# Inverse transform of a gated convolution in three classes of time points, with the filter taken through the path of the activations and a gate ahead of the weight loads

## The chip, the cores and the metric

The kernel runs on 1 core of one Trainium2 chip. The metric is the device time of one execution in microseconds (us). The time before is the median of 3 runs, 191.38 us (190.6 to 192.84). The profile is of one further execution.

## What is computed

Attention first, then a convolution whose result is gated by two projections. B = 4 batches, H = 8 heads, S = 768 positions, D = 64, model width 512. Heads 0, 2 and 6 attend causally to everything, the other five to 4 sink positions and a window of 64. The convolution is circular over the 768 positions, with one filter per channel, and is computed on the spectrum.

```python
scores = scale * np.matmul(q, k.transpose(0, 1, 3, 2))
scores = np.where(mask[None, :, :, :], scores, -1000000000.0)
a = np.exp(scores - max); a = a / sum
x = np.matmul(a, v)                       # -> [B, S, 512]
...
x1, x2, x3 = split(x @ w_proj, 3)         # w_proj 512 x 1536
X2 = np.fft.rfft(x2, n=S, axis=1)
H = np.fft.rfft(filter_fft, n=S, axis=0)[None, :, :]
x2_conv = np.fft.irfft(X2 * H, n=S, axis=1)
return (x1 * x2_conv * x3) @ w_out        # [4, 768, 512] float32
```

## The kernel before, in words

**Order.** The order of all work is written out by hand in two strings of words. `AHEAD` (L121) is what runs before a branch that asks whether the heads have the expected kinds; `FAST` (L126) is the rest. Each word is the name of a small function; the kernel calls them one by one (L1738), and every engine works through its own instructions in that order, with semaphores between engines. `@4` names a PSUM bank, `/v`, `/s` and `/p` name VectorE (DVE), ScalarE (ACT) or GpSimd (POOL). Helpers `ev` (L969, a copy out of PSUM or a cast), `two` (L977, an operation on two tensors) and `scale` (L1157) take the engine from that letter, so that many operations share the lines 971, 973, 975 and 978.

**Attention.** Sixteen pairs of heads (n = 0 to 15, four per batch) are loaded by `lq`, `lk`, `lv` on SP's queue, cast (`cq`, `ck`, `cv`), turned (`T`, `E`), multiplied (`sc`, L1452), masked by a bias matmul (`sb`, L1465, n below 4) or by a multiplication (`mk`), exponentiated on ACT (`ex`, L1471), multiplied by the values (`at`, L1516) and normalized (`rec`, `nm`, L1533; twice by ACT, L1530). Buffers of a head pair are two or three deep.

**Transform forwards.** The normalized heads are folded over the half length (`fd`, `fe`) and over sixths (`fA`, `fS`, `fb`, `fr`, L1561), and three matmuls per half (`W`, L1569 to L1573) give 2 x 384 frequencies per channel, copied out by `We`. Heads are also turned for the two projections (`tn`, `te`): by PE (L1589) for the head pairs in `TURNED_BACK`, by a DMA for the others. `X` (L1620) multiplies the spectrum by the middle third of w_proj, so that frequencies lie on the partitions, and `Xe` copies it out.

**The filter.** `lfilt` (L1236) loads it on POOL's queue, as `lw` (L1244) and `lwo` (L1249) load the weights; their place in the order is all that sets when they start. `fold0` and `fold1` fold it, 18 matmuls of 512 columns (`F`, L1265) with the table G as weights give its spectrum with frequencies on the partitions, and `H` (L1272, L1274, with two copies by DMA, L1288 and L1292) scales it into HAB.

**Product and inverse.** `pa`, `pb`, `pc` multiply X by HAB into P; for one tile of three the halves of X have to be exchanged by two DMAs (`sw`, L1645). For each of four blocks of 128 channels, `c` (L1685) makes two chains of three matmuls with 384 columns, one even and one odd under a shift by half the length. `ce` copies the one out on ACT, and `cv` adds and subtracts the other on DVE (L1696). `y` multiplies by x1, `g` (L1674, L1678) by x3; x1 and x3 come from `x1`, `x3` (L1655), and `o` (L1712) with `oe` and `st` gives the output.

```python
INVERSE = (((1, 0, 3), (1, 1, 4), (2, 1, 5)), ((0, 0, 0), (0, 1, 1), (2, 0, 2)))
```

The table Gi of the inverse is the transpose of the table G: 18 transposes on PE (`Gt`, L1227) and three copies (`Ge`). G itself is mixed from one wave by four operations on DVE (`Gm`, L1188). `blank` words are matmuls on zeros (L1041) near the start.

Of the kernel before, what the change touches and what calls it, by code (L numbers as in the profile page):

```python
# [114 lines left out]
TURNED_BACK = (0, 1, 2, 3, 4, 5, 6, 7, 14, 15)  # L115
# [3 lines left out]
BLANKS = (5, 2, 2, 2, 2, 2, 2, 2, 2, 2, 2, 2, 2)  # L119

AHEAD = """  # L121
lflag lk0 lq0 lk1 lq1 mblank want tcol fcol0 table sin0 fcol1 blank0@6 tfrac quarter mtab0 par turns other angle
ident mtab1 wrap size sin cos
# [3 lines left out]
ones1 ones2 mtab3 blank5@0 lq2 lk2 blank10@1 ck0/v skew0/s lv0 parb skew1/p G32/s T0.1@2 xp0 cq0/v lk3 blank6@3  # L127
mtab2 E0.1/v lv1 blank8@4 Gk1/s lv3 blank7@5 Gm00 btab G31/p blank1@6 ck1/v kz1 lq3 T0.0@7 lk4 alt blank3@0 Gm2
cq1/s G30/p Gh0 lq4 T1.1@1 Gm01 kz0 lv2 E0.0/s G00/v T1.0@3 G01/p Gm1 cq2/s lk6 E1.1/v sc0.1@4 sb0.1 lq6 ck2/p
sc0.3@6 ex0.1 Gh1 E1.0/v sc0.4@0 ones0 kx1/p sb0.4 lk5 sb0.3 T2.1@2 ex0.4 kz2 lk7 sc0.0@4 E2.1/v lq5 cv0/p sb0.0  # L130
Gt1@3 ex0.3 lq7 blank2@0 kx2/v Gt2@1 Gk0/p ex0.0 lv6 T2.0@2 ks1/p Ge2/v ck3/p sc0.2@6 Ge1/s E2.0/v sc1.2@4 sb1.2
lfilt sb0.2 T3.1@0 ex1.2 sc0.5@2 Gt0@1 ex0.2 cv1/v sc2.3@4 E3.1/v lv4 vx1/p sb0.5 ex0.5 sc1.0@6 lw2.1 Ge0/v
sb1.0 ks2/s vs1/v at0.0@2 lw2.0 ex1.0 at0.1 cq3/v lw0.1 T3.0@0 ex2.3 kx3/v sc1.1@6 rec0 lw1.1 sb1.1 nm0/v cv3/s
blank11@1 ex1.1 sc2.1@4 fe0/p sb2.1 tn0@1 cq4/v E3.0/s at1.0@2 lw0.0 blank9@6 ex2.1 ks3/v sc2.4@6 ck4/v at1.1
lw1.0 ex2.4 T4.0@0 T4.1@4 vs3/v E4.0/s te0/v lwo sc3.1@6 sb3.1 rec1 E4.1/s nm1/v fd0/p sc3.2@0 sb3.2 ex3.1 fe1/v
tn1@5 fS0/p ex3.2 sc3.0@2 fold0/v sb3.0 sc2.0@6 ex3.0 vx3/v fd1/v F0.0@4 fA0/v fA1/p F0.1@0 H0.0/s fS1/v fb0/p
sb2.0 fold1/v sc2.2@2 H0.1/s sb2.2 ex2.0 fb1/p te1/v F1.0@1 fr1 ex2.2 F2.1@4 fr0 cv2/v H1.0/s F2.0 lv5 vs2/v
vx2/p H0.2/v at2.0@6 H2.0/s at2.1 ck6/p sc4.0@2 H2.1/s rec2 Hd0 at3.0@0 nm2/v at3.1 H2.2/s lk9 rec3 fe2/p F1.1@6
nm3/v ex4.0 Hd1 T6.1@7 fd2/p H1.1/v sc4.5@4 sc4.4@0 ex4.5 tn2@2 fe3/v ex4.4 fd3/v tn3@3 te2/v sc4.2@4 te3/v
ex4.2 mk4.2/p W1.0@0 E6.1/v W1.1 blank4@2 We1/s ks6/v sc4.1@4 fS3/p blank12@3 ex4.1 fA3/v sc4.3@0 fr3 x10.3.0@2  # L140
fb3/p cq6/s mk4.0/v W0.0@4 W0.1 ex4.3 lq9 x10.3.1 ck7/v ck5/s x30.0.0@0 We0/v fS2/p lk10 kx6/s T7.1@7 cq5/p
xs0.3/s x10.0.1@4 H1.2/s fA2/v lq8 x10.0.0 fb2/v E7.1/s fr2 mk4.1/v W3.0@2 lk8 cq7/s T5.0@6 xs0.0/v ks7/p
x30.0.1 E5.0/s lq10 kx7/v W3.1 cv6/v T7.0@7 We3/s T5.1@4 vs6/v lv9 vx6/p g0.0 T6.0@5 E7.0/s W2.1@2 W2.0 E6.0/v
cv4/p E5.1/s x10.1.0@0 We2/v kx5/s ks5/p lv7 at4.0@6 sc5.1@4 cv5/s sc5.0@2 H2.3 at4.1 H2.4 ex5.1 lv8 vx5/p
x10.1.1 rec4 vs5/p nm4/v ex5.0 sc5.2@4 ex5.2 sc6.0@6 H2.5 sc6.3@2 mk5.1/v ex6.0 X0.0.1@4 mk5.0/v mk5.2/v ex6.3
X0.0.0 mk6.0/v fe4/v xs0.1/s fd4/v sc7.1@6 sc6.1@2 fS4/v Xe0.0/s fA4/v sc7.0@0 fr4 ex6.1 pa0.0/v at5.0@4 at5.1
fb4/v mk6.1/p ex7.0 X0.1.1@2 rec5 nm5/v X0.1.0 ex7.1 fe5/v mk7.0/v X0.2.1@0 cq8/s fd5/v mk7.1/v Xe0.1/s sc7.2@4
sc6.4@6 X0.2.0 fA5/p ex7.2 ck10/v sc6.2@2 pa0.1/v Xe0.2/s tn4@4 pb0.1/v tn5@5 ex6.2 sw0.1 W4.0@0 mk7.2/v W4.1
sw0.0 ck8/v x10.2.0@2 We4/s pc0.1/v T8 cq10/s mr6/v x30.1.0@0 mk6.2/v ck9/s x30.1.1 fS5/v pa0.2/v T10 ex6.4
x10.2.1 fb5/p g0.1 cv7/s at6.0@6 cq9/s vx7/v x30.2.1@0 te5/v xs0.2/s fr5 T9 x30.2.0 vs7/v cv8/s W5.1@2 pb0.2/v  # L150
# [778 lines left out]
def patterned(tc, pools, pre, q, k, v, flags, n_sink, window, moe_w_proj, moe_filter_fft, moe_w_out, out):  # L929
# [903 lines left out]
```

## Time and profile before

| | |
|---|---|
| median of 3 runs | 191.38 us (190.6 to 192.84) |
| the profiled execution | 190.34 us, of which the span of its instructions is 188.6 us |
| mean granted clock of TensorE | 0.985 |
| busy in the span | PE 176.5, DVE 161.1, ACT 145.7, POOL 68.5 us |
| DMA | 34.06 MB, mean 181 GB/s |

The page of the profile gives the busy time of each engine; the view of stretches gives the same for chosen parts of the span; the view by line and form groups instructions of one kind and gives their busy time, then the mean duration of one in ns, and after the second bar the idle time before them. Instructions of one engine can overlap by some tens of ns at their ends, and matmuls more, so that the busy time of a group can be less than its count times its mean. The chain of waits lists the pieces of the chain of work that ended last: start, length, engine, line.

### The profile page before, as it was taken

To read this page: it belongs to the slowest core of one execution; us is meant where nothing else is said; L and a number is where in the kernel's file an instruction comes from. 1 tells how busy PE (TensorE), PEld (TensorE's weight loads), DVE (VectorE), ACT (ScalarE), POOL (GpSimd) and SP (SyncE) were. 2 spreads that over 40 slices of the span, in tenths; PEclk is the share of its full clock that TensorE was granted. 3 is DMA by queue.
4 is the path that set the end of the run, shared out by engine and by line. 5 is a ranking of instruction groups with operands and counts; after the bars stand their busy time and mean duration, and the time that the engine had idled before them with its cause. 6 is when DMAs were issued, how large, how long until landed. Compare 5 with 4: busy or idle time off the path is not lost.

```text
span 188.6 us, 4479 instructions
## 1 busy us (share of the span) xinstructions
PE 176.5 (94%) x1694; PEld 103.5 (55%) x1694; DVE 161.1 (85%) x329; ACT 145.7 (77%) x210; POOL 68.5 (36%) x103
## 2 busy tenths in 40 slices
PE   6989999989998999999999999999999999999970
PEld 2446664647745563575555656655657765455420
DVE  6886799889979999999979999999899996499810
ACT  5887899999999999988989999696976331435350
POOL 5884785554322224570250450600741630000000
PEclk9988999999999999999999999999999999999997
DMA  4999999999999999999999989922262002412083
GB/s 161 332 270 283 206 196 239 271 292 240 219 198 229 210 210 171 218 220 194 231 244 254 217 250 225 214 47 50 82 76 111 3 2 113 146 24 111 37 299 126
DMA packets 78960, 34.06 MB, mean 181 GB/s; under 512 B 68306, under 2 KB 75218, under 8 KB 78930
## 3 DMA queue, kind: packets, MB, share of 16 engines
q1 hardware_dynamic: 75986, 30.81, 72.8%
q0 software_dynamic: 2944, 2.88, 9.1%
q8 instruction: 15, 0.25, 0.6%
q14 instruction: 15, 0.12, 0.3%
HBM read 24.64 MB, written 6.29 MB: 164 GB/s over the span
## 4 chain that ended last, share of the span: by engine, by line
PE 67%; ACT 14%; DVE 11%; issue 3%; POOL 2%; DVEq 0%; ACTq 0%; POOLq 0%
PE space L1655 19%; PE space L1712 11%; PE space L1620 8%; PE space L1452 7%; PE space L1685 7%; PE space L1516 6%; ACT f_pT L1471 5%; ACT f_HAB L1274 3%; PE space L1465 2%; PE space L1569 2%; DVE f_attn L1533 1%; PE space L1571 1%; ACT f_xh L975 1%; DVE r_P L978 1%; PE space L1407 1%
## 5 line engine op out<-in xcount | busy, mean ns | idle before, releaser
L1471 ACT ACTIVATE f_pT<-space 128x1024 bf16<-128x1024 f32 (+3 forms) x68 | 58.8, 917 | 6.3 <-PE space L1465 2.1
L1655 PE MATMUL space<-f_xT,f_wproj 128*128 128x384 bf16 x256 | 47.9, 326 | 0.1
L1655 PEld LDWEIGHTS <-f_wproj 128*128 128x128 bf16 x256 | 24.0, 98 | 17.0 <-issue 1.0
L1712 PE MATMUL space<-f_wout,r_gy 128*128 128x512 bf16 x96 | 24.7, 379 | 0.0
L1452 PE MATMUL space<-f_qkT 64*128 64x128 bf16 (+3 forms) x248 | 22.4, 252 | 1.2 <-DVE f_qkT L971 0.6
L1620 PE MATMUL space<-f_wproj,f_xh 128*128 128x512 bf16 x96 | 22.7, 379 | 0.1
L1685 PE MATMUL space<-f_Gi,r_P 128*128 128x384 bf16 x96 | 19.1, 326 | 0.6 <-ACT f_evs L975 0.3
L978 DVE TENSOR_TENSOR f_pT<-f_pT,r_mtab 128x1024 bf16<-128x1024 bf16 (+3 forms) x33 | 18.5, 585 | 1.0 <-ACT f_pT L1471 0.8
L975 ACT COPY f_o<-space 128x1024 f32<-128x1024 f32 (+1 forms) x12 | 9.9, 836 | 11.3 <-PE space L1712 11.2
L1516 PEld LDWEIGHTS <-f_pT 128*128 128x128 bf16 x472 | 16.6, 97 | 3.6 <-issue 0.9
L1516 PE MATMUL space<-f_v_aug,f_pT 128*128 128x65 bf16 x392 | 17.9, 193 | 0.6 <-ACT f_X L975 0.5
L978 POOL TENSOR_TENSOR f_uv<-f_fo 128x256 bf16<-128x256 bf16 x12 | 9.1, 765 | 23.3 <-DVE f_fo L978 19.0
L1452 PEld LDWEIGHTS <-f_qkT 64*128 64x128 bf16 x248 | 10.3, 94 | 13.1 <-issue 10.4
L1696 DVE TENSOR_TENSOR f_conv<-f_evs,space 128x384 bf16<-128x384 f32 x32 | 16.1, 547 | 0.6 <-PE space L1685 0.3
L975 ACT CAST f_xh<-space 128x768 bf16<-128x768 f32 x14 | 11.2, 808 | 4.9 <-PE space L1573 4.6
L1620 PEld LDWEIGHTS <-f_xh 128*128 128x128 bf16 x96 | 9.0, 97 | 10.0 <-issue 0.4
L1712 PEld LDWEIGHTS <-r_gy 128*128 128x128 bf16 x96 | 9.0, 98 | 8.9 <-issue 0.4
L1533 DVE TENSOR_TENSOR f_attn<-space,f_rec 128x768 bf16<-128x768 f32 x14 | 13.4, 955 | 0.4
L1685 PEld LDWEIGHTS <-r_P 128*128 128x128 bf16 x96 | 8.8, 97 | 7.3 <-DVE r_P L978 0.9
L978 POOL TENSOR_TENSOR f_fo<-f_attn 128x384 bf16<-128x384 bf16 x11 | 10.4, 957 | 2.4 <-DVE f_attn L1533 1.9
L975 ACT CAST f_X<-space 128x1024 bf16<-128x1024 f32 x8 | 8.2, 1019 | 2.8 <-PE space L1620 2.0
L978 POOL TENSOR_TENSOR f_pT<-f_pT,r_mtab 128x512 bf16<-128x512 bf16 (+1 forms) x6 | 6.7, 1117 | 9.5 <-ACT f_pT L1471 9.5
(136 smaller groups left out, 346.2 us busy)
## 6 DMA issues: line engine op xcount, KB each, us to landing
f_v_f<-in_v_dram SPq DMA_DIRECT2D x32, 192.0 KB, 4.8
out_dram<-f_o SPq DMA_DIRECT2D x9, 512.0 KB, 2.9
r_qk_f<-in_k_dram SPq DMA_DIRECT2D x10, 192.0 KB, 4.5
r_qk_f<-in_q_dram SPq DMA_DIRECT2D x10, 192.0 KB, 5.3
r_qk_f<-in_k_dram SPq DMA_DIRECT2D x4, 384.0 KB, 11.4
r_qk_f<-in_q_dram SPq DMA_DIRECT2D x4, 384.0 KB, 6.0
f_qk_f<-in_q_dram SPq DMA_DIRECT2D x4, 384.0 KB, 5.5
f_qk_f<-in_k_dram SPq DMA_DIRECT2D x4, 384.0 KB, 6.6
```

What stands on the lines that cost most here:

```text
L975: nc.scalar.copy(out=out, in_=in_)
L978: (nc.gpsimd if now["engine"] == "p" else nc.vector).tensor_tensor(out, a, b, op)
L1274: nc.scalar.activation(out=out_(), in_=in_(), func=AF.Copy, scale=w / S)
L1452: nc.tensor.matmul(sc[:, bank, col:col + 128 * cnt], lhsT=keys, rhs=qkT(n)[rows, 0, 128 * i:128 * (i + cnt)], start=(col == 0 or not biase ...
L1471: nc.scalar.activation(out=pT(n)[:, c, :, 0:w], in_=held[f"sc.{n}.{c}"][:, :, 0:w], func=AF.Exp, scale=SCALE)
L1516: nc.tensor.matmul(att[:, hh, 65 * i:65 * i + 65], lhsT=pT(n)[:, c, bank, col:col + 128], rhs=values, start=(z == 0), stop=(z == len(here) ...
L1533: nc.vector.tensor_mul(attn(n).rearrange("p i hh d -> p hh i d"), rows[:, :, :, 0:64], held[f"rec.{n}"][:, :, :, None].to_broadcast([128, ...
L1620: nc.tensor.matmul(ps[:, u, :], lhsT=xh(b)[:, cc, chain, 128 * part:128 * part + 128], rhs=wproj()[:, cc, DM:2 * DM], start=(cc == 0), sto ...
L1655: nc.tensor.matmul(ps[:, s, 0:HS], lhsT=wproj()[:, cc, part * DM + cb * 128:part * DM + (cb + 1) * 128], rhs=xT(b)[:, cc, s * HS:s * HS + HS],
L1685: nc.tensor.matmul(ps[:, 0, 0:HS], lhsT=P(b)[:, t, u, ch], rhs=Gi()[:, tile_no], start=(m == 0), stop=(m == 2))
L1696: fn(conv[:, half * HS:half * HS + HS], held[f"evs.{b}.{cb}"], held[f"c_ps.{b}.{cb}.1"][:, 0, 0:HS])
L1712: nc.tensor.matmul(ps, lhsT=gy(b)[:, cb, i * 128:(i + 1) * 128], rhs=wout()[:, cb, :], start=(cb == 0), stop=(cb == NC - 1))
```

## The change

The inverse no longer has two chains of three matmuls. The spectrum of a batch is kept in six groups of 128 rows: real and imaginary parts of the frequencies w, 256 + w and 256 - w, where w runs over the multiples of 3. Nine operations per batch (`qa` to `qm`) join P on these rows, with sums and differences SD, a factor KAPPA and a separate tile Y0, so that each of three classes of time points (the positions 3i, 3i + 1, 3i + 2, up to a shift) needs only two matmuls with 256 columns. One PSUM tile of 768 columns then holds the whole convolution of a channel block, and one copy `cv` on ACT, written with a step of three elements, replaces `ce` and the two `cv`.

The tables become smaller: G has one tile of 128 rows instead of three, Gi and Gj are read straight from the wave (`Gi0`, `Gi1`, `Gz`, `Gj`), and `Gm`, `Gh`, `Gt`, `Ge` go. The wave has 512 columns instead of 384, so the operations ahead of the branch are a third wider.

The filter now takes the path of the activations: folds, then `fAF`, `fSF`, `fbF`, `frF` over all 512 channels, `K` (eight words of three matmuls), four copies `Ke`, and 24 transposes on PE (`F0` to `F2`) that bring the frequencies back to the partitions. The copies `We` and `Ke` write with a step of two elements. The DMAs `Hd` and `sw` go.

`gate` is a copy of one element on POOL that reads the loaded q of head pair 3; `lfilt`, `lwo` and all `lw` stand behind it on POOL's queue.

Both strings are new. Head pair 14 is turned by a DMA instead of PE, `nm` is done by DVE every time, and masks, casts, multiplications `y` and copies are dealt out anew among DVE, ACT and POOL.

```diff
-TURNED_BACK = (0, 1, 2, 3, 4, 5, 6, 7, 14, 15)
+TURNED_BACK = (0, 1, 2, 3, 4, 5, 6, 7, 15)
...
-lflag lk0 lq0 lk1 lq1 mblank want tcol fcol0 table sin0 fcol1 blank0@6 tfrac quarter mtab0 par turns other angle
-ident mtab1 wrap size sin cos
+lflag lk0 lq0 lk1 lq1 mblank want tcol fcol0 fcol1 fcol4 table sin0 fcol2 fcol3 blank0@6 tfrac quarter mtab0 par
+turns other angle ident mtab1 wrap size sin cos
...
+sc2.3@4 ex1.1 cq3/v gate sc2.1@6 sb2.1 lfilt kx3/s at1.0@0 ck4/s at1.1 at0.1 lw0.0 rec1 nm1/v ex2.1 rec0 fd1/p
...
+ex4.4 T5.0@2 tn0@3 lw2.1 lq10 ex4.0 vx3/v sc4.2@0 lw2.0 ck6/v ex4.2 sc3.2@6 fold0/v sb3.2 lk9 E5.0/s sc4.1@0
...
-    G = C("G", [128, 6, NM, 128], BF16)
-    Gi = C("Gi", [128, 6, NM, 128], BF16)
+    G = C("G", [128, 6, 128], BF16)
+    Gi = C("Gi", [128, 2, 4, 128], BF16)
+    Gj = C("Gj", [128, 2, 256], BF16)
...
+    @op("gate")
+    def _():
+        nc.gpsimd.tensor_copy(out=buf("gate", [1, 1], FP32), in_=held["qk_f32.3"][0:1, 0, 0, 0, 0:1])
...
-                for m in range(NM):
-                    nc.tensor.matmul(ps, lhsT=Gh()[:, m] if tile_no is None else G()[:, tile_no, m, :],
-                                     rhs=fold()[:, chain, m, :], start=(m == 0), stop=(m == NM - 1))
...
+    def spectrum(ps, u, uv, br, ch):
+        nc.tensor.matmul(ps[:, u, 0:256], lhsT=br[:, 1, u, ch], rhs=G()[:, 3 * u:3 * u + 2], start=True, stop=False)
+        nc.tensor.matmul(ps[:, u, 0:256], lhsT=uv[:, 2 * u, ch], rhs=Gk()[:, u], start=False, stop=True)
+        nc.tensor.matmul(ps[:, u, 256:384], lhsT=br[:, 0, u, ch], rhs=G()[:, 3 * u + 2], start=True, stop=True)
+
+    def sorted_(x, ps):
+        ev(x.rearrange("p g (j u) -> p u g j", u=2), ps[:, :, 0:HS].rearrange("p u (g j) -> p u g j", g=6))
...
+            for c, g in enumerate(SPECTRUM[t]):
+                for cc in range(NC):
+                    nc.tensor.transpose(ps[:, 0, DM * c + 128 * cc:][:, 0:128], Hx()[:, cc, g], identity())
...
-        for half in range(2):
-            @op(f"sw{b}.{half}")
-            def _(b=b, half=half):
-                Xw = buf(f"Xw.{b}", [128, 2, DM], BF16, "Xw")
-                to, at = slice(64 * half, 64 * half + 64), slice(64 - 64 * half, 128 - 64 * half)
-                nc.sync.dma_start(out=Xw[to], in_=held[f"X.{b}.2"][at])
+        @op(f"qa{b}")
+        def _(b=b):
+            two(SD(b)[:, 0:2], P(b)[:, 1], P(b)[:, 2], ALU.add)
+
+        @op(f"qs{b}")
+        def _(b=b):
+            two(SD(b)[:, 2:4], P(b)[:, 1], P(b)[:, 2], ALU.subtract)
+
+        @op(f"qr{b}")
+        def _(b=b):
+            scale(SD(b)[0:1], flat(b)[0:1, 2:6], 2.0)
+
+        @op(f"qh{b}")
+        def _(b=b):
+            scale(Y0(b), P(b)[:, 0], 0.5)
+
+        @op(f"qz{b}")
+        def _(b=b):
+            two(Y0(b), Y0(b), SD(b)[:, 0:4:3], ALU.add)
+
+        @op(f"qd{b}")
+        def _(b=b):
+            scale(SD(b)[:, 1:3], SD(b)[:, 1:3], 2.0 * KAPPA)
+
+        @op(f"qb{b}")
+        def _(b=b):
+            two(P(b)[:, 0], P(b)[:, 0], SD(b)[:, 0:4:3], ALU.subtract)
+
+        @op(f"qp{b}")
+        def _(b=b):
+            two(flat(b)[:, 2:4], P(b)[:, 0], SD(b)[:, 1:3], ALU.add)
+
+        @op(f"qm{b}")
+        def _(b=b):
+            two(flat(b)[:, 4:6], P(b)[:, 0], SD(b)[:, 1:3], ALU.subtract)
...
-            for r in range(2):
-                @op(f"c{b}.{cb}.{r}")
-                def _(b=b, cb=cb, r=r, ch=ch):
-                    ps = banks(f"c_ps.{b}.{cb}.{r}", count=1)
-                    for m, (t, u, tile_no) in enumerate(INVERSE[r]):
-                        nc.tensor.matmul(ps[:, 0, 0:HS], lhsT=P(b)[:, t, u, ch], rhs=Gi()[:, tile_no],
-                                         start=(m == 0), stop=(m == 2))
-
-            @op(f"ce{b}.{cb}")
-            def _(b=b, cb=cb):
-                ev(buf(f"evs.{b}.{cb}", [128, HS], FP32, f"evs{cb % 2}"), held[f"c_ps.{b}.{cb}.0"][:, 0, 0:HS])
-
-            for half, fn in ((0, nc.vector.tensor_add), (1, nc.vector.tensor_sub)):
-                @op(f"cv{b}.{cb}.{half}")
-                def _(b=b, cb=cb, half=half, fn=fn):
-                    conv = buf(f"conv.{b}.{cb}", [128, S], BF16, f"conv{cb % 2}")
-                    fn(conv[:, half * HS:half * HS + HS], held[f"evs.{b}.{cb}"], held[f"c_ps.{b}.{cb}.1"][:, 0, 0:HS])
+            @op(f"c{b}.{cb}")
+            def _(b=b, cb=cb, ch=ch):
+                ps = banks(f"c_ps.{b}.{cb}").rearrange("p a f -> p (a f)")
+                for s, (re, im) in enumerate(POINTS):
+                    for c, rows in enumerate((re, im)):
+                        rhs = Gi()[:, c].rearrange("p a f -> p (a f)")[:, START[s]:START[s] + 256] if s else Gj()[:, c]
+                        nc.tensor.matmul(ps[:, 256 * s:256 * s + 256], lhsT=rows(b)[:, ch], rhs=rhs,
+                                         start=(c == 0), stop=(c == 1))
+
+            def inward(x):
+                return x.rearrange("p (i s) -> p s i", s=3)
+
+            if (b, cb) not in DIRECT:
+                @op(f"cv{b}.{cb}")
+                def _(b=b, cb=cb, inward=inward):
+                    conv = buf(f"conv.{b}.{cb}", [128, S], BF16, f"conv{cb % 2}")
+                    ps = held[f"c_ps.{b}.{cb}"].rearrange("p a f -> p (a f)")
+                    ev(inward(conv), ps[:, 0:S].rearrange("p (s i) -> p s i", s=3))
```

More of the change, by code (lines that the diff above doesn't have):

```diff
@@ L1298, in _, with sixths @@
[L1298 to L1304 removed]
+        two(fold()[:, 1], filt()[:, 0:NM, :], filt()[:, NM:NT, :], ALU.subtract)
+    def sixths(name, fo, uv, br):
+        @op("fA" + name)
+        def _():
+            two(uv()[:, 1:3], fo()[:, :, 1], fo()[:, :, 2], ALU.add)
+        @op("fS" + name)
+        def _():
+            two(uv()[:, 0:4:3], fo()[:, :, 2], fo()[:, :, 1], ALU.subtract)
+        @op("fb" + name)
+        def _():
+            two(br()[:, 0], fo()[:, :, 0], uv()[:, 1:4:2], ALU.add)
+        @op("fr" + name)
+        def _():
+            nc.vector.scalar_tensor_tensor(out=br()[:, 1], in0=uv()[:, 1:4:2], scalar=-0.5, in1=fo()[:, :, 0],
+                                           op0=ALU.mult, op1=ALU.add)
```

377 lines of the change are left out of this document (171 added, 206 removed).

## The prediction, made before the changed kernel ran

> **What bounds the kernel now.** I read the page's totals first, then the busy time by stretch, then the chain of waits.
>
> ```profile
> span 188.6 us, 4479 instructions
> PE 176.5 (94%) x1694; PEld 103.5 (55%) x1694; DVE 161.1 (85%) x329; ACT 145.7 (77%) x210; POOL 68.5 (36%) x103
> ```
>
> ```profile
> 0.00:20.00 20.00, 17.13 (x130) 8.89 (x131) 15.46 (x40) 14.79 (x22) 13.73 (x37) 0.91 0.95 260
> 20.00:80.00 60.00, 56.81 (x670) 34.92 (x669) 54.85 (x110) 58.88 (x81) 27.27 (x35) 1.00 1.16 223
> 100.00:130.00 30.00, 30.00 (x289) 17.41 (x285) 29.40 (x61) 26.29 (x44) 8.50 (x9) 1.00 0.88 188
> 80.00:146.90 66.90, 66.90 (x690) 40.25 (x689) 63.47 (x136) 57.26 (x89) 23.30 (x28) 1.00 0.83 171
> 146.90:182.60 35.70, 35.68 (x210) 19.41 (x207) 27.35 (x46) 14.23 (x19) 4.25 (x6) 1.00 0.24 85
> 182.60:188.60 6.00, 0.00 (x0) 0.00 (x0) 0.00 (x0) 0.59 (x1) 0.00 (x0) 0.81 0.47 170
> ```
>
> The columns are PE, PEld, DVE, ACT, POOL, the granted clock, DMA share, GB/s. PE leads in the total, but not everywhere. From 20 to 80 us ACT is busy 58.88 of 60, 98.1%. From 80 us PE never stops, and DVE beside it reaches 29.40 of 30, 98%, between 100 and 130. Only after 146.9 us, where the last attention matmul ends, does PE stand alone: DVE 27.35 of 35.7, ACT 14.23. So time saved on PE is worth its full price in the last stretch; before it, two other engines have little left. The chain of waits (start, length) gives the ends of the stretches and the step of a matmul:
>
> ```profile
> 28.14 0.34 PE space L1589 x6
> ...
> 114.27 1.95 PE space L1685 x12
> ...
> 145.26 1.65 PE space L1516 x54
> ...
> 177.40 5.19 PE space L1712 x24
> ```
>
> A step is 5.19/24 = 0.216 us with 512 columns, 1.95/12 = 0.163 with 384, 0.34/6 = 0.056 with 128; on that line 256 columns take 0.109.
>
> **The change part by part.** The rows that price it (busy time of the group, mean ns of one):
>
> ```profile
> L1696 DVE TENSOR_TENSOR f_conv<-f_evs,space 128x384 bf16<-128x384 f32 x32 | 16.1, 547 | 0.6 <-PE space L1685 0.3
> L1533 DVE TENSOR_TENSOR f_attn<-space,f_rec 128x768 bf16<-128x768 f32 x14 | 13.4, 955 | 0.4
> L975 ACT CAST f_xh<-space 128x768 bf16<-128x768 f32 x14 | 11.2, 808 | 4.9 <-PE space L1573 4.6
> L978 DVE TENSOR_TENSOR r_P<-r_P,f_m 128x1024 bf16<-128x1024 bf16 x12 | 8.2, 687 | 0.1
> L975 ACT CAST f_X<-space 128x1024 bf16<-128x1024 f32 x8 | 8.2, 1019 | 2.8 <-PE space L1620 2.0 <-DVE r_P L978 0.7
> L971 DVE COPY f_qkT<-space 128x768 bf16<-128x768 bf16 x8 | 7.6, 950 | 0.7 <-PE space L1407 0.7
> L1561 DVE SCALAR_TENSOR_TENSOR f_br<-f_uv,f_fo 128x256 bf16<-128x256 bf16 x16 | 7.0, 445 | 0.3
> L975 ACT COPY f_evs<-space 128x384 f32<-128x384 f32 x14 | 6.8, 496 | 3.0 <-DVE f_conv L1696 2.1 <-PE space L1685 0.8
> L975 ACT CAST f_v_aug<-f_v_f 128x768 bf16<-128x768 f32 x8 | 6.7, 841 | 0.5 <-PE space L1516 0.5
> L978 DVE TENSOR_TENSOR f_pT<-f_pT,r_mtab 128x512 bf16<-128x512 bf16 x10 | 5.2, 527 | 0.2
> L1530 ACT ACTIVATE f_attn<-space,f_rec 128x64 bf16<-128x64 f32 x24 | 5.1, 344 | 0.0
> L1227 PE MATMUL space<-r_identity,r_G 128*128 128x128 bf16 x18 | 1.9, 252 | 0.0
> L1188 DVE SCALAR_TENSOR_TENSOR r_G<-r_P,f_skew 128x256 bf16<-128x256 f32 x4 | 1.8, 459 | 0.0
> L971 DVE COPY f_Gi<-space 128x768 bf16<-128x768 bf16 x2 | 1.1, 554 | 1.5 <-PE space L1227 1.5
> L1146 DVE TENSOR_SCALAR r_gy<-r_gy 128x384 int32<-128x384 int32 x1 | 0.6, 562 | 0.0
> L1129 DVE TENSOR_SCALAR f_btab<-r_mtab 128x896 bf16<-128x896 bf16 x1 | 0.4, 393 | 0.4 <-POOL r_mtab L1113 0.4
> ```
>
> PE, whole run: the 96 inverse matmuls go from 384 to 256 columns, 96 x (0.163 - 0.109) = -5.2. The 18 transposes of the table go: 1.0 at 0.056, 1.9 by their group's busy time, I take -1.4. The filter's 18 matmuls of 512 (3.9) become 16 of 256, 8 of 128 and 24 transposes (1.7 + 0.4 + 1.3 = 3.4), -0.5. Head pair 14 turned by DMA, -0.3. Together -7.4. Counting both orders up to the last attention matmul, 6.7 of it falls before that point; the work behind it goes from 35.8 to 35.2.
>
> ACT, up to the same point, numbers of instructions by the two orders: 10 fewer `ce` at 6.8/14 (-4.9); 8 `cv` of 768 columns, priced as `We` at 11.2/14 = 0.80 (+6.4); the normalizations that DVE takes, 24 x 5.1/24 (-5.1); 3 `Ke` at 0.80 (+2.4); `H` from five of 1024 and two of 512 columns to two and four, at 1.02 and 0.5 (-2.1); one `qd`, two `qh` at 1.02 (+3.1); 5 more casts and copies of 768 columns (+4.0), 2 more `oe` (+2.0), small ones (+1.5). Sum +7.3. Over the whole run it is +12, but the rest falls where ACT is free.
>
> DVE, likewise: 22 `cv` at 16.1/32 and 2 `ce` go (-12.1). Three batches of the joining come before that point: 17 operations on 1024 columns at 0.687 (+11.7), 6 scalings at 0.393 per 896 columns, those of one row and 2048 columns at most 0.9 (+3.3). The filter's sixths: three at 0.687, one like L1561 with four times the columns, 1.3 (+3.4). Tables: four L1188 and two `Ge` go (-2.9), `Gh` for small new ones of its size. Three `nm` from ACT at 0.955 (+2.9), four masks from POOL (+1.8), 2 `E` at 0.95 (+1.9), `Ke` and `H` (+2.0), other moves, mostly to ACT and POOL (-5.8). Sum about +6, of +7 over the run. POOL loses 8; it has 64% free.
>
> Ahead of the branch three operations in a row on DVE grow by a third of 0.56 or less: +0.4 on the start, uncovered.
>
> Now the stage up to the last attention matmul. ACT needs 14.8 + 58.9 + 57.3 + 7.3 = 138.2, DVE 15.5 + 54.9 + 63.5 + 6 = 139.8, PE 140.8 - 6.7 = 134.1. If after the first 20.4 us each keeps the best rate that it shows now, ACT is through at 20.4 + 123.4/0.981 = 146.2 and DVE at 20.4 + 124.3/0.98 = 147.2, against 146.9 now. PE alone would be through at 140.2. So the cover of PE's saving is gone: what is late next is DVE, with ACT one microsecond behind.
>
> The nine joining operations run between the last `pc` and the first `c` of a batch, where `pc` alone stood. In the last batch the order puts 40 matmuls of 512 and 24 of 384 columns between the end of X3.2 and c3.0, 12.5 us, and DVE has there a copy (1.2), 15 operations at 0.687 and a wait for one scaling on ACT (1.0), also 12.5: just covered, 0 to 1 us; I take 0.3. Behind c3 one copy of 0.80 per block on ACT replaces three shorter steps; PE has x33.3 and o3 meanwhile, cost 0. The transfers `sw` and `Hd` go; PE did not wait for them, gain 0.
>
> The gate:
>
> ```profile
> f_wproj<-in_moe_w_proj_dram POOLq DMA_DIRECT2D x6, 256.0 KB, 11.2
> r_gy<-in_moe_filter_fft_dram POOLq DMA_DIRECT2D x1, 768.0 KB, 11.7
> ...
> 14.66 1.06 POOL L1236 DMA_DIRECT2D r_gy<-in_moe_filter_fft_dram  x1
> 19.75 0.55 DVE L971 CAST f_qk_bf<-f_qk_f 128x768 bf16<-128x768 f32 x1
> 27.88 0.95 DVE L978 TENSOR_TENSOR r_gy<-r_gy 128x1536 bf16<-128x1536 bf16 x1
> ```
>
> The filter's load starts at 14.66 now and is folded at 27.88. The gate sits behind the cast of q3 (19.75 now); with 11.7 to land, the filter is there at about 33. On POOL only small copies and the loads queue behind the gate. The new order folds where ACT has some 29 us of work behind it, which at 14.8 by 20.4 us and 98.1% from there is 35 us. Cost 0, at most 3 if it lands late, since then DVE waits; a gain of up to 1 from head loads that meet fewer weights. I take 0.
>
> Sum: 147.2 + 0.3 + 35.2 + 6.0 for the tail = 188.7, against 188.6. The profiled execution took 190.34, 1.74 beyond its span, and the median of the runs is 1.04 above that, so the median comes to 191.5.
>
> A copy with stepped output appears nowhere now. Nearest is the cast that writes runs of 64 into rows of 65, 841 ns against 808. I take no cost; the bound is twice the time, 24 copies x 0.8 = 19 us on ACT by that point. The Trainium skill, SBUF — State Buffer, in the box on SBUF cachelines, says that at least two hits in a line of 16 bytes keep full bandwidth; by that rule steps of 4 and 6 bytes cost nothing and the sum is the same. No run here shows it yet.
>
> **The rivals.**
>
> Faster: DVE's extra work slips behind the last attention matmul, where it has 8 us free; 5 us of it, the joining of batch 2, is not needed by attention at all. Then only the whole run binds DVE: 20.4 + (161.1 + 7 - 15.5)/0.98 + 6 = 182, and PE gives 188.6 - 7.4 = 181.2. With a microsecond of waits the span is 183 and the median 186. Against it: each engine works in the written order.
>
> Slower: the joining makes DVE's work a chain of dependent operations in front of PE, and its rate falls. From 20 to 146.9 us it is 118.3 of 126.9 = 93% now. At 94.5% the stage ends at 20.4 + 124.3/0.945 = 151.9, the span is 193.4, the median 196. It decides below about 96.5%. Against it: PE set the pace then.
>
> Slower by the shared port:
>
> ```profile
> L978 DVE TENSOR_TENSOR f_uv<-f_fo x20: 280/289/849, 29.4 to 150.9; 128x256 bf16<-128x256 bf16 x20
> L978 DVE TENSOR_TENSOR r_P<-r_P,f_m x12: 678/687/693, 65.0 to 169.9; 128x1024 bf16<-128x1024 bf16 x12
> ```
>
> ```profile
> L978 DVE TENSOR_TENSOR f_uv<-f_fo 128x256 bf16<-128x256 bf16 x20 | 7.5, 392 | 0.1
> ```
>
> Minimum, median and longest of one: some f_uv operations take three times the shortest, the joining's model r_P never. The change replaces additions with one operand in PSUM by such operations wholly in SBUF. That group of 20, busy 7.5 us in all, loses 7.5/20 - 0.28 = 0.095 us on each; 29 operations of the joining and the filter then lose 2.8 us, span 191.5, median 194.3.
>
> The Trainium skill, SBUF — State Buffer, section SBUF: two separate sides, says that a DVE instruction with two SBUF inputs and a GpSimd instruction that reads SBUF lock each other out. The f_uv row agrees; the r_P row shows nothing of it.
>
> Stepped copies at twice the time: span over 200.
>
> **How the numbers follow.** Forecast 0.36, faster rival 0.28, chain 0.24, port 0.07, steps 0.05. About 1%, 1.9 us, is what a measurement of this kernel can tell from no change. The forecast's own range is 189.6 to 193.3. Faster takes its rival and a little of the forecast's low edge, 0.29; same 0.36; slower the other three, 0.35. The range of 8 in 10 goes from the faster rival's centre to the chain's, 186 to 196.5, leaving the outer halves of both out.
>
> **What would show it.** Right: ACT and DVE both above 96% from 20 us to the last attention matmul, which still ends near 147; PE idle 5 to 8 us in that stretch; PE 169 busy. Wrong: the last attention matmul before 144 (faster) or after 149 with DVE waiting on its own r_P and f_SD (chain); the L975 copy into f_conv over 0.9 us (steps); f_SD with maxima far above 0.69 (port).

## The result, and the profile after

The changed kernel takes 202.62 us (201.53 to 204.17, 4 runs) against 191.08 us before (190.6 to 192.84, 4 runs): a ratio of 1.063, 95% interval 1.054 to 1.072. The forecast was 191.5 in a range of 186.0 to 196.5, so it is slower by 11.5 us and outside the range. The profiled execution took 204.17 us, its span is 202.5.

The page's totals and two of its rows by slices, after:

```profile
span 202.5 us, 4406 instructions
PE 174.4 (86%) x1683; PEld 107.8 (53%) x1700; DVE 168.5 (83%) x330; ACT 169.2 (84%) x206; POOL 63.5 (31%) x95
PE   6899786699789998767799999998899999999680
PEclk9999999669999999979999999999999999999998
```

DVE's 168.5 is the forecast sum (161.1 + 7). ACT's 169.2 is not: 145.7 + 12 = 157.7 was forecast, 11.5 less. PE has holes in the first half that it did not have before, and its granted clock drops twice. The same two rows of the kernel before:

```profile
PE   6989999989998999999999999999999999999970
PEclk9988999999999999999999999999999999999997
```

Busy time by stretch, after (columns as in the prediction), up to the last attention matmul and behind it:

```profile
0.00:157.90 157.90, 138.53 (x1468) 87.10 (x1483) 138.89 (x279) 143.66 (x182) 61.76 (x93) 0.97 0.89 181
157.90:196.50 38.60, 35.18 (x217) 20.57 (x217) 29.59 (x52) 24.43 (x23) 1.72 (x2) 1.00 0.29 83
```

The first stretch ends at 157.9 instead of the forecast 147.2, the second takes 38.6 instead of 35.2. Groups by line and form, after; the third row is a plain copy of the same size, for comparison:

```profile
L974 ACT CAST f_conv<-space 128x768 bf16<-128x768 f32 x16 | 22.0, 1464 | 4.0 <-PE space L1708 4.0
L974 ACT CAST f_xh<-space 128x768 bf16<-128x768 f32 x14 | 14.3, 1026 | 3.8 <-PE space L1272 3.8
L974 ACT CAST r_x1s<-space 128x768 bf16<-128x768 f32 x8 | 6.6, 822 | 0.9 <-PE space L1529 0.5 <-PE space L1677 0.4
...
L977 DVE TENSOR_TENSOR f_SD<-r_P 128x1024 bf16<-128x1024 bf16 x7 | 4.8, 701 | 0.0
...
L970 DVE CAST f_xh<-space 128x768 bf16<-128x768 f32 x2 | 2.1, 1027 | 0.0
```

The copy with a step of three elements takes 1464 ns where 0.80 us was forecast, the one with a step of two 1026. The joining takes the forecast time (701 against 687, the longest 823, where its rival wanted maxima far above 690), so the rival of the shared port is out. The chain of waits, after:

```profile
90.63 1.29 PE space L1708 x6
...
157.26 0.67 PE space L1529 x22
157.93 0.67 PE space L1708 x6
158.63 1.46 ACT f_conv L974
...
160.98 2.75 ACT f_conv L974 x2
```

The chain now runs through `cv` (ACT f_conv), which the forecast had at 0.80 us each and off the path. The same six matmuls of the inverse take 1.29 us at 90.63 and 0.67 at 157.93: the granted clock is 0.50 from 90 to 91 us.

Three theories were put to the test. A: the stepped copies on ACT make the difference. B: the joining on DVE does, and the copies are covered. C: the late weights do. In the experiments, at8 stands for the end of the attention matmuls of head pair 8 in the trace (81.8 us before, 90.6 after), and so on for other head pairs.

### The profile page after: what moved, and what is told of

Same layout as the page of the kernel before. It is cut to its first block, busy times and chain, and to the rows that moved or that the text cites. A ratio compares the mean times of both kernels' runs of the same rounds, so it can differ in the third digit from the quotient of the medians.

```text
span 202.5 us, 4406 instructions
## 1 busy us (share of the span) xinstructions
PE 174.4 (86%) x1683; PEld 107.8 (53%) x1700; DVE 168.5 (83%) x330; ACT 169.2 (84%) x206; POOL 63.5 (31%) x95
## 4 chain that ended last, share of the span: by engine, by line
PE 41%; ACT 24%; DVE 14%; DMA 9%; issue 6%; POOL 2%; SPq 1%; ACTq 0%; DVEq 0%
PE space L1677 9%; ACT f_conv L974 8%; PE space L1739 8%; DMA f_qk_f<-in_k_dram 7%; ACT f_pT L1484 7%; PE space L1613 5%; PE space L1529 5%; PE space L1465 3%; DVE r_P L977 3%; PE space L1708 2%; PE space L1270 2%; PE space L1042 2%; PE space L1271 2%; PE space L1420 2%; DVE f_qkT L970 1%
## 5 line engine op out<-in xcount | busy, mean ns | idle before, releaser
L1739 PE MATMUL space<-f_wout,r_gy 128*128 128x512 bf16 x89 | 23.1, 379 | 2.8 <-DVE r_gy L1700 1.5
L974 ACT CAST f_conv<-space 128x768 bf16<-128x768 f32 x16 | 22.0, 1464 | 4.0 <-PE space L1708 4.0
L977 DVE TENSOR_TENSOR f_pT<-f_pT,r_mtab 128x512 bf16<-128x512 bf16 (+3 forms) x37 | 20.7, 567 | 1.3 <-ACT f_pT L1484 1.2
L1529 PEld LDWEIGHTS <-f_pT 128*128 128x128 bf16 x472 | 18.2, 102 | 6.2 <-DVE f_pT L977 2.2
L974 ACT CAST f_xh<-space 128x768 bf16<-128x768 f32 x14 | 14.3, 1026 | 3.8 <-PE space L1272 3.8
L1546 DVE TENSOR_TENSOR f_attn<-space,f_rec 128x768 bf16<-128x768 f32 x16 | 15.2, 956 | 0.4
L977 POOL TENSOR_TENSOR f_br<-f_fo,f_uv 128x256 bf16<-128x256 bf16 x7 | 5.2, 744 | 21.8 <-DVE f_uv L977 13.8
L1420 PE MATMUL space<-r_identity,f_qk_bf 128*128 128x128 bf16 x96 | 8.5, 230 | 4.1 <-DVE f_qk_bf L970 1.7
L977 DVE TENSOR_TENSOR r_gy<-f_conv,r_gy 128x768 bf16<-128x768 bf16 x12 | 6.7, 556 | 6.4 <-ACT f_conv L974 6.4
L1270 PE MATMUL space<-r_G,f_br 128*128 128x256 bf16 x32 | 9.3, 290 | 2.1 <-ACT f_conv L974 1.0
```

What stands on the lines that cost most here:

```text
L974: nc.scalar.copy(out=out, in_=in_)
L977: (nc.gpsimd if now["engine"] == "p" else nc.vector).tensor_tensor(out, a, b, op)
L1270: nc.tensor.matmul(ps[:, u, 0:256], lhsT=br[:, 1, u, ch], rhs=G()[:, 3 * u:3 * u + 2], start=True, stop=False)
L1420: nc.tensor.transpose(ps[:, 0, t * 128:(t + 1) * 128], qk_bf(n)[:, a, t].rearrange("p hh d -> p (hh d)"), identity())
L1529: nc.tensor.matmul(att[:, hh, 65 * i:65 * i + 65], lhsT=pT(n)[:, c, bank, col:col + 128], rhs=values, start=(z == 0), stop=(z == len(here) ...
L1546: nc.vector.tensor_mul(attn(n).rearrange("p i hh d -> p hh i d"), rows[:, :, :, 0:64], held[f"rec.{n}"][:, :, :, None].to_broadcast([128, ...
```

## The experiments

### The step, and the weights' places

**e1_output_order**: same result, the copies run in the order of their output.

```diff
-        ev(x.rearrange("p g (j u) -> p u g j", u=2), ps[:, :, 0:HS].rearrange("p u (g j) -> p u g j", g=6))
+        ev(x.rearrange("p g (j u) -> p g j u", u=2), ps[:, :, 0:HS].rearrange("p u (g j) -> p g j u", g=6))
...
-                    ev(inward(conv), ps[:, 0:S].rearrange("p (s i) -> p s i", s=3))
+                    ev(conv.rearrange("p (i s) -> p i s", s=3), ps[:, 0:S].rearrange("p (s i) -> p i s", s=3))
```

> The copies cv, We and Ke move the same elements to the same places, but run in the order of their output: they write without a step and read PSUM with one (256 words for cv, a bank for We and Ke). Theory A, the step in the write costs ACT its time (1464 ns for cv against 0.82 for a plain copy of this size, 1026 against 0.81 for We): cv falls to about 0.85 us and We to 0.82, ACT saves 16 x 0.64 + 17 x 0.21 = 13.9 us, and DVE takes over as the bound: span 191 to 195 against 202.5. Theory A2, a step costs on either side: no copy changes by more than 0.2 us and the time stays at 202. Theory B, the joining on DVE holds everything and the copies are covered: cv falls as in A, but the span falls by less than 3 us.

193.8 us, ratio to before 1.020 (1.011 to 1.030). Totals and groups by form, then the stretches, and the end of the attention on the chain:

```profile
PE 170.4 (89%) x1683; PEld 105.5 (55%) x1700; DVE 166.4 (87%) x330; ACT 156.9 (82%) x206; POOL 64.8 (34%) x95
```

```profile
L974 ACT CAST f_conv<-space 128x768 bf16<-128x768 f32 x16 | 12.2, 810 | 3.0 <-PE space L1708 3.0
L974 ACT CAST f_xh<-space 128x768 bf16<-128x768 f32 x14 | 11.2, 802 | 4.7 <-PE space L1272 4.6
L970 DVE CAST f_xh<-space 128x768 bf16<-128x768 f32 x2 | 1.9, 954 | 0.0
```

```profile
0.00:150.00 150.00, 135.30 (x1467) 84.71 (x1482) 137.02 (x279) 136.82 (x182) 63.08 (x93) 0.98 0.95 190
150.00:185.10 35.10, 34.62 (x219) 20.74 (x219) 29.39 (x52) 19.26 (x23) 1.72 (x2) 1.00 0.32 93
```

```profile
149.42 0.67 PE space L1529 x22
```

Theory A holds: 8.8 of the 11.5 us, by the medians, come from the step in the write. The copies still read with a step, now on the side of PSUM (256 words for `cv`, a bank for `We`), and that costs nothing: 810 and 802 ns here, 810 and 802 with no step on either side in e3.

**e2_cv_unstepped**: in the changed kernel, only `cv` is written anew, `ev(conv, ps[:, 0:S])`; the order of the time points is left out.

> cv alone without any step, neither in reading nor in writing: the time points of the convolution stay sorted by class, which leaves that part of the computation out. Prices the step of cv alone. Theory A: cv 0.82 us, ACT saves 10.3 us in all, 5 to 8 of it before the last attention matmul and 3 to 4 behind it; span 194 to 197. Theory B: cv falls likewise, span above 199.5.

194.84 us: `cv` at 809 ns, We left at 1026. The step of `cv` alone is worth 7.8 us.

**e3_no_steps**: `cv` as in e2, and We and Ke write `"p g (u j) -> p u g j"`.

> cv, We and Ke without any step on either side: time points stay sorted by class and frequencies by parity, both left out of the computation. The best that the removal of the steps can give. Theory A: cv 0.82, We 0.81, ACT 155 busy instead of 169; the last attention matmul ends at 147 to 151 instead of 157.8, span 190 to 194. Theory B: span above 199.5.

193.96 us, the same as e1 within the runs: the stepped read leaves nothing to gain.

**e4_early_weights**: in the changed kernel, the gate gone, `lfilt` ahead of `vs1/p`, and all weights behind `ks3/p`; of the line of the order:

```diff
-... sc1.1@0 ks3/p sb1.1 ...
+... sc1.1@0 ks3/p lw0.0 lw0.1 lw1.0 lw1.1 lw2.0 lw2.1 lwo sb1.1 ...
```

> The gate is gone and the loads stand where they stood before: the filter at about 14 us, the weights in one group at about 19. Theory C, the late filter and weights are what costs time (ACT waits 5 us in all between 20 and 80 us): ACT idle there falls to 2 us and the span by 2 to 4 us. Theories A and B: the time stays within 1 us of 202.5, or gets worse by up to 2 us since the head loads meet all weights at once.

215.83 us, 13.2 more than the changed kernel: theory C falls, and by a price none of the theories had. One stretch, and the chain, of this kernel:

```profile
20.00:40.00 20.00, 6.52 (x82) 4.03 (x78) 4.24 (x7) 6.39 (x9) 4.21 (x7) 0.76 1.18 236
```

```profile
21.80 17.72 DMA f_qk_f<-in_q_dram
39.54 0.57 DVE f_qk_bf L970
```

All three engines are busy a third of the time or less: everything waits for q4, which is issued after filter and weights and lands 17.72 us later.

### What is left: 3 us more than before

e1 is the base of the next runs. Its stage to 150 us carries less than was forecast on ACT (136.8 against 138.2) and DVE (137.0 against 139.8), and still ends 3 us later than before. The interval of e1's ratio (1.011 to 1.030) is 2 us wide on either side, so a difference of less than that between e1 and one run is not told apart; where it matters the ratio to the kernel before is given.

**e5_one_engine_per_table**: HAB becomes three tiles; four words change engine, `H0.3` and `H1.2` from `/s` to `/v`, `H2.2` and `H2.4` from `/v` to `/s`.

> From the kernel with output order (span 191.1, last attention matmul 150.0). The filter's spectrum HAB becomes three tiles and all scalings into one tile stand on one engine, so that ACT and DVE no longer wait for each other's writes (1.6 us of DVE and 1.5 us of ACT idle between 48 and 58 us). Theory W, part of the lost 3 us comes from waits ahead of 80 us: span falls by 1 to 2 us. Theory D, only the load of DVE counts: within 0.5 us.

193.38 us, 0.4 less, which the runs do not tell apart. In the profiled executions, from at3 to at5 it gains 1.4 us (19.5 against 20.9), and from at7 to at8 it takes 0.7 longer (13.5 against 12.8): half of what was saved is given back.

**e6_no_joining**: the words `qa` to `qm` dropped, and

```diff
-    POINTS = ((lambda b: Y0(b)[:, 0], lambda b: Y0(b)[:, 1]),
+    POINTS = ((lambda b: flat(b)[:, 0], lambda b: flat(b)[:, 1]),
```

> From the kernel with output order, without the nine joining operations of each batch: P goes straight into the inverse, so the joining is left out of the computation. Removes 23 additions of 0.69 us and 3.7 us of scalings from DVE (19.6) and 6.1 from ACT; some 14.5 of DVE's lie before the last attention matmul. Theory D, DVE is the bound from 80 us on and the joining is what it pays for the smaller inverse: last attention matmul at 141 to 144, span 181 to 185. Theory W, the loss lies before 80 us, where little joining is done: last attention matmul above 147, span above 188.

192.83 us, 1.0 less than e1 (ratio 1.012, 1.007 to 1.017, against 1.020). The last attention matmul ends at 149.4, not at 141 to 144: theory D (DVE is the bound), and with it B, falls. The stretches of this kernel:

```profile
80.00:100.00 20.00, 18.92 (x193) 11.91 (x192) 15.98 (x41) 19.95 (x29) 2.78 (x4) 0.91 1.26 213
100.00:150.00 50.00, 50.00 (x514) 29.95 (x509) 41.39 (x89) 44.07 (x55) 9.60 (x11) 1.00 0.58 122
```

With DVE relieved, ACT is full to 100 us (19.95 of 20) and PE without a gap behind it.

**e7_c_half_longer**: in `c`, `for again in range(2 - c):` ahead of the matmul, with `start=(c + again == 0)`.

> From the kernel with output order: each block of the inverse issues nine matmuls of 256 columns instead of six, three of them twice (which counts that part twice and changes the result), so that PE gives back the 5.2 us that the change took from it. Theory D, PE is not the bound before the last attention matmul: that point moves by less than 1 us, and only the seven blocks behind it (7 x 0.33 = 2.3) count: span 192.5 to 194. Rival, PE still sets the pace: span 196 or more.

199.37 us, 5.6 more for 5.2 us of matmuls: the rival, PE sets the pace, holds behind at8. In the trace 2.1 us are lost before the first block of the inverse, where nothing was changed (at8 at 89.7 against 87.6). From there to the last attention matmul 2.6 us of added matmuls cost 1.8 (64.3 against 62.5), and the 2.6 us behind it (eight blocks, not the seven of the expectation) cost 2.5 (43.5 against 41.0).

**e8_class0_on_pe**: `qh`, `qz` and Y0 go.

```diff
-        scale(Gj(), Gi()[:, :, 0:2].rearrange("p c a f -> p c (a f)"), 2.0)
+        scale(Gj(), Gi()[:, :, 0:2].rearrange("p c a f -> p c (a f)"), 3.0)
...
-                    for c, rows in enumerate((re, im)):
+                    for c, rows in enumerate(parts):
-                        rhs = Gi()[:, c].rearrange("p a f -> p (a f)")[:, START[s]:START[s] + 256] if s else Gj()[:, c]
+                        rhs = Gi()[:, c].rearrange("p a f -> p (a f)")[:, START[s]:START[s] + 256] if c < 2 else Gj()[:, c - 2]
```

with P0' = P0 - S and S as four row groups in the first entry of POINTS.

> From the kernel with output order, same result: the first class of time points uses 0.5 (P0 - S) + 1.5 S in place of 0.5 P0 + S, so that Y0 with its scaling and its addition goes (DVE 4 x 0.69 + 3 x 0.42 = 4.0 us, ACT 1.1) and PE makes two more matmuls of 256 columns per block (32 x 0.109 = 3.5). Theory D: the last attention matmul comes 2 to 3 us earlier, the seven blocks behind it cost 1.5 us: span 189 to 191. Theory P, PE sets the pace: span 193 or more.

195.38 us; at 1.023 (1.017 to 1.030) not told apart from e1. Theory D, with 189 to 191, falls, and the span of 193.9 lies where theory P has it: 5.1 us less on DVE and ACT gain nothing when PE gets 3.5 more.

**e9_casts_on_pool**: `cv7 cv8 cv9 cv10 cq11 ck11` from `/s` to `/p`.

> From the kernel with output order (span 191.1), where PE is busy 99% and more from 100 us on, but sits idle 11 us between 20 and 100, 8 more than in the kernel before. Six casts of 0.84 us (cv7 to cv10, cq11, ck11) go from ACT to POOL, 5.0 us of ACT between 66 and 90 us. Theory E, ACT is what PE waits for there: at9 comes 2 to 4 us earlier (100.5 now) and the span falls as much. Rival, it is the written order of ACT and DVE together, or loads: span within 1 us.

197.66 us, 3.9 more (ratio 1.035, 1.030 to 1.041), where 2 to 4 less was expected: a miss for theory E.

**e10_no_gate_op**: the word `gate` dropped, the loads stay.

> From the kernel with output order, without the gate's copy; the weight loads keep their places in the order. POOL works on ks3 until 18.7 us anyway, and the gate ended its wait at 18.8. If the place in the order is what holds the loads back, nothing changes (span within 0.7 us of 191.1); if the gate is, the loads start earlier and lq4 lands late as in the run with early weights (span 195 and more).

194.46 us; at 1.018 (1.012 to 1.023) not told apart from e1's 1.020. The place of the loads in the order does what the gate was to do.

**e11_before_narrow_c**: in the kernel before,

```diff
-                        nc.tensor.matmul(ps[:, 0, 0:HS], lhsT=P(b)[:, t, u, ch], rhs=Gi()[:, tile_no],
+                        nc.tensor.matmul(ps[:, 0, 0:256], lhsT=P(b)[:, t, u, ch], rhs=Gi()[:, tile_no, 0:2],
```

> The kernel before with nothing changed but the 96 matmuls of the inverse, which write 256 columns instead of 384 (a third of the result is left out; the copies still read 384). PE loses 96 x 0.054 = 5.2 us. The forecast's step says that DVE and ACT then set the pace: last attention matmul at 145 to 147, span 185.5 to 187. Rival, PE's saving comes through in full in the old order: span 183.4.

189.68 us, ratio 0.993 (0.989 to 0.996): of 5.2 us less on PE, 1.2 arrive, and the rival (all of it) falls. Two stretches of it, to and from the last attention matmul (147.9 in this execution, whose head pair 2 came 2.2 us later):

```profile
80.00:147.00 67.00, 65.61 (x669) 40.50 (x678) 64.24 (x139) 59.07 (x95) 23.32 (x29) 1.00 0.92 177
147.80:183.00 35.20, 34.23 (x208) 19.14 (x209) 27.68 (x47) 13.88 (x19) 4.69 (x6) 1.00 0.23 82
```

PE, without a gap before, now has gaps: others hold it at almost the old pace, also in the last stretch (35.2 against 35.7, by one execution of each).

**e12_later_weights**: `lw1`, `lw2` behind `fb0/p`, `lwo` behind `fb3/p`.

> From the kernel with output order: lw1 and lw2 are issued at about 37 us and lwo at about 51, instead of between 24 and 31, so that the head loads k4 to q7 share the transfer engines with the filter and lw0 alone. Theory F, late head loads cost PE its idle time in 20 to 40 us (4.3 us idle; a load of k took 11.7 us to land): at3 (40.3 now) comes 1 to 3 us earlier, span 188 to 190. Rival: other waits take its place, or X and x3 wait for their weights at 56 to 60: span 190.5 and more.

194.37 us (ratio 1.020, 1.014 to 1.026), no gain: theory F falls.

**e13_no_filter** and **e14_before_no_filter**: the filter's words dropped in e1 and in the kernel before, `HAB()[:, t, 0:2]` and `[:, t, 2:4]` replaced by `wout()[:, 0:2]` and `[:, 2:4]`.

> From the kernel with output order, without the filter's path (folds, sixths, K, Ke, F, H; X is multiplied by rows of w_out instead, so the filter is left out of the computation; its load stays). Takes DVE 10 us, ACT 7 and PE 3.4 out of the stretch from 33 to 57 us. Theory G, the new filter path is what holds the kernel back ahead of 88 us: at8 (87.4 now) comes 5 us earlier or more and the span falls by 4 to 6, clearly more than the same cut gives in the kernel before. Theory O, it is the written order as a whole: the two cuts give the same within 1 us.

> The kernel before, without its filter path (folds, 18 matmuls of 512 columns, H and its two DMAs; w_out's rows in their place, so the filter is left out of the computation; its load stays). Takes PE 3.9, ACT 6.3 and DVE 4.6 us out. Theory G: 1 to 3 us faster than before. Theory O: as much as the cut in the other kernel, within 1 us.

192.07 and 190.71 us: 1.7 less than e1, and nothing in the kernel before (ratio 0.998, 0.993 to 1.003). Theory G's price of 4 to 6 us is a miss; its sign is right as far as 1.7 us can be told (ratio 1.009, 1.006 to 1.012, against 1.020): the new path costs something, the old one nothing. at8 comes at 86.8 only.

**e15_four_casts_on_pool**: e5 with `cv7` to `cv10` on POOL.

> From the kernel with output order and one engine per table (median 193.4): the casts of v7 to v10 alone go from ACT to POOL, 3.4 us of ACT between 66 and 88 us; q11 and k11, which stood on the way to the exponentials in the run with six casts (197.7), stay on ACT. Theory E, ACT holds PE there: median 190 to 192. Rival: ACT's load does not count there, within 1 us of 193.4, or slower where POOL's casts come late.

195.54 us, at a ratio of 1.028 (1.021 to 1.035), where e5 has 1.014 (1.008 to 1.021). The runs of the two overlap (192.99 to 196.71, and 192.44 to 194.27), so how much slower it is stays open. No run comes to the 190 to 192 of theory E, which falls.

**e16_early_weights_q4_first**: e4 with `lq4` right behind `lk4`.

> From the kernel with early weights (median 215.8; stepped copies): only the load of q4 is issued right behind k4 and ahead of k7 and v2, as the kernel before has it, so that it does not stand behind the filter. There it landed 17.7 us after its issue, and PE, DVE and ACT all waited for it until 39.5 us. Theory C2, the gate saves this one wait: median 202 to 206. Rival, early weights delay all head loads: 210 and more.

214.61 us. C2 falls; the chain of this kernel shows the rival at work, since v2 is now what lands late:

```profile
17.38 19.91 DMA f_v_f<-in_v_dram
```

**e18_no_joining_casts_on_pool** and **e17_no_joining_no_filter**: e6 with the four casts on POOL, and e6 with the cut of e13.

> The kernel without the joining, and in addition the casts of v7 to v10 on POOL. Without the joining DVE stood idle from 82.6 to 84.9 us, since the copy of v10's rows waits for its cast, which stands in ACT's full queue, and the mask of head pair 8 is behind that copy. Theory T, ACT and DVE take turns as what holds PE between 74 and 88 us, so that relief of one alone is lost: with both relieved at8 comes at 83 to 85 (86.95 without the joining, 87.52 with the four casts alone), and the median falls from 192.8 to 190 or less. Rival, something else pins at8: within 1 us of 192.8.

> Both cuts together: no filter path (192.1 alone) and no joining (192.8 alone); both are left out of the computation. Theory T: DVE is relieved twice and ACT's queue stays full between 78 and 92 us, so the two savings (1.7 and 1.0) add at most: median 190.5 to 191.5. Rival, DVE is the one engine that counts: 188 or less.

193.58 and 190.88 us. The first is not faster than e6, with at8 at 88.1: that ACT and DVE hold PE by turns, so that relief of both must pay, is not borne out by casts that go to POOL. The second is 2.9 below e1, about the sum of the two cuts (1.7 + 1.0), at a ratio of 1.000 (0.995 to 1.006) to the kernel before.

Of the kernels that leave nothing out of the computation none beats the kernel before; the best of them is e5, at 1.014 (1.008 to 1.021).

## Why the prediction was wrong, step by step

**The step that failed: "A copy with stepped output appears nowhere now. ... I take no cost."** The term of the sum was 0.80 us for each `cv` and each `We`; the runs showed 1464 ns and 1026 ns, and 810 and 802 once the write had no step (e1). The nearest row, 841 ns against 808, was no neighbour: it steps once in 64 elements, `cv` at every one. The bound of twice the time came close (1464 against 810 is 1.8 times), but no row had given it, so that was luck; it stood in the rivals with a chance of 0.05 and a span over 200, and the span is 202.5. The prediction's own sign for it, a copy into f_conv over 0.9 us, came true.

In the profiled executions the stage to the last attention matmul ends at 157.9 with the step and at 150.1 without, and the work behind it takes 38.6 or 35.1: 7.8 + 3.5 us of the span. That is more than the 8.8 us between the medians: the profiled executions took 204.17 us (median 202.62) and 192.83 (median 193.8).

The Trainium skill, SBUF — State Buffer, in the box on SBUF cachelines, asks for two hits in a line of 16 bytes; steps of 4 and 6 bytes give two to four, and cost 28% and 81% here. The measurement decides, and it goes against the rule. One row could not exclude the bound, and the chance of 0.05 for it was too small. Why the cost grows as it does with the step is not shown.

**"cost 0" behind c3** failed with it: in the last batch four copies of 1.46 us stand in one row on ACT, and o3 cannot cover them, since most of it waits for the last one. From the chains, the first piece of the inverse and the output matmuls that end the wait, after and in e1:

```profile
185.47 0.67 PE space L1708 x6
193.17 4.07 PE space L1739 x18
```

```profile
176.11 0.67 PE space L1708 x6
181.50 4.07 PE space L1739 x18
```

It is 7.7 us from one to the other with the step and 5.4 without. With 0.81 us a copy the forecast 35.2 is met (35.1).

**The loads of the engines** were nearly right otherwise. In e1, to the last attention matmul: ACT 136.8 (138.2 forecast), DVE 137.0 (139.8), PE 135.3 (134.1).

**"each keeps the best rate that it shows now", 98%,** failed too, and this is the 3 us that are left in e1. There ACT gets through its 136.8 us in 150, that is (136.8 - 16.1)/130 = 93% behind the first 20 us, and DVE through its 137.0 at (137.0 - 15.9)/130 = 93% as well, the rate that the slower rival had worked out for the kernel before. The best rate of one engine in one stretch is not what three coupled engines keep over a whole stage. By the medians the runs give 1.0 of the 3 us to the joining and 1.7 to the new filter path (by the ratios 1.7 and 2.2), and both cuts together leave no difference to the kernel before. The joining's chain was the slower rival, with 196 us; the joining costs a fifth to a third of the 4.7 us of span that it was given.

**PE's saving is eaten**: right, and more than was said. In the kernel before, 5.2 us less on PE are worth 1.2 (e11), although PE shows no gap there from 80 us on. "its full price in the last stretch" failed: 27 matmuls, four blocks and a half, should give 27 x 0.054 = 1.5, and gave 0.5. The reverse does not hold: of work added to PE most is paid (e7).

**The gate, "cost 0":** right as far as the runs go: without the gate's copy (e10) and with later weights (e12) the time stays. "a gain of up to 1 from head loads that meet fewer weights" says nothing near what the late loads are worth in the new order: with all weights early the kernel is 13.2 us slower, and moving q4 ahead only hands the wait to v2.

**What stays open.** How the work of joining and filter path turns into 2.9 us is not settled. In e1 PE is idle 11 us between 20 and 100 us, ACT and DVE some 6 to 8 each. No single cut (e6, e13) and no relief of ACT by POOL (e9, e15) moved at8 below 86.8 us; both cuts together moved it to 84.3, against 81.8 in the kernel before. Which of the waits in that stretch is the first cause cannot be told from the cuts.

The falling clock (below) was suspected, and no run kept PE busy with blank matmuls in the gaps. Against it speaks that from at7 to at8 e17 takes 11.95 us without a fall and e6 11.6 with one, and that the earlier fall, between 36 and 40 us, is in e17 too, which is no slower than the kernel before. And in e1, right behind the slow matmuls, PE waits for a mask from DVE, so that faster ones would only have waited longer:

```profile
86.25 1.31 PE L1529 MATMUL space<-f_v_aug,f_pT 128*128 128x65 bf16 x37 [0.95 <-DVE f_pT L977]
```

## What to carry to other kernels

A copy that reorders should run in the order of its output: let the read from PSUM take the steps, and the write be contiguous. An engine that shows no gap need not be the only bound: cut its work in the old kernel (a few narrower matmuls are enough) before building on the saving. And when only a bound prices an operation, and that operation stands on an engine at 98%, the bad end deserves a chance of its own size, not the remainder.

## What the runs showed of the hardware

Copies by ACT of 128x768 from PSUM into SBUF in bf16: 802 to 810 ns with no step in the write (e1), 1026 with a step of 4 bytes and 1464 with 6 (after). DVE pays less for 4 bytes: 1027 ns (after) against 954 (e1). Reads from PSUM with a step of 1 KB in the inner loop cost ACT nothing (`cv`, 810 ns in e1 and 809 in e2, which reads without one).

TensorE's granted clock fell to half after stretches that were only thinly filled, with no long gap in them. A stretch of e1 in which the clock was at half, with the same length before it; the timeline of PE around them; and for comparison two stretches of that length in e17:

```profile
77.31:80.72 3.41, 1.69 (x17) 0.88 (x17) 3.41 (x7) 3.41 (x5) 2.07 (x2) 1.00 0.95 201
80.72:84.14 3.42, 3.42 (x11) 1.61 (x11) 3.23 (x9) 3.42 (x5) 0.00 (x0) 0.50 1.15 208
```

```profile
78.19 0.39 PE L1465 MATMUL space<-f_qkT 64*128 64x512 bf16 x2 [0.42 <-ACT f_pT L1484]
79.10 0.34 PE L1465 MATMUL space<-f_qkT 64*128 64x384 bf16 x2 [0.52 <-ACT f_pT L1484]
80.02 0.50 PE L1465 MATMUL space<-f_qkT 64*128 64x512 bf16 x6 [0.58 <-ACT f_pT L1484]
80.72 4.42 PE L1677 MATMUL space<-f_xT,f_wproj 128*128 128x384 bf16 x16 [0.20 <-ACT f_pT L1484]
```

```profile
80.68:84.09 3.41, 2.04 (x47) 1.66 (x46) 1.28 (x4) 3.19 (x7) 0.91 (x1) 1.00 1.02 205
84.09:87.50 3.41, 3.02 (x31) 2.02 (x28) 3.05 (x8) 3.41 (x6) 0.82 (x1) 1.00 1.08 224
```

In e1 PE was busy 1.69 of 3.41 us (50%), with gaps of 0.4 to 0.6 us. The 16 matmuls behind them take 0.276 us each instead of 0.163, at half clock for the first 3.42 us. In e17 PE was busy 2.04 of 3.41 us (60%), with one gap of 1.37 us, and the clock stayed. So in these two places the filled share went with the fall, and the longest gap did not. Where the exact limit lies is not shown. The Trainium skill, TensorE: Matmul & The Clock Gate, Part 1, lets the clock fall to half after an idle window of about 3.4 us; the half agrees, a gap of that length is nowhere in this stretch.
